# Head gates by one broadcast load, a planner that keeps TensorE's tilings apart, and copies that free PSUM first on VectorE

## The chip, the cores and the metric

The kernel runs on one core of one Trainium2 chip. The metric is the device time of one execution in microseconds (us), the median over several runs. The engines named below are TensorE (PE: matrix products; its weight loads are shown apart as PEld), VectorE (DVE), ScalarE (ACT), GpSimd (POOL) and SyncE (SP, which only issues DMAs and waits). Each engine executes its own instructions strictly in the order in which the program gives them; engines and DMAs wait for one another by semaphores. SBUF is the on-chip memory with 128 partitions, PSUM the accumulator memory that TensorE writes, in banks of 128 x 512 fp32.

## The reference

Two branches read the same x of shape (1, 2048, 512) and are mixed token by token:

```python
g = sigmoid((x * gate_w).sum(-1, keepdims=True))
out = g * A(x) + (1 - g) * B(x)
# B: a gated feed-forward, F = 1792
B = (relu(x @ W_gate) * (x @ W_up)) @ W_down
# A: 32 heads of 16, the sequence cut into 4 segments of 512
for s in range(4):
    a_dot = softmax(q_s k_s^T / 4 + causal mask) v_s
    a_mem = phi(q_s) M / (phi(q_s) z + 1e-6)      # phi(t) = t + 1 if t > 0 else exp(t)
    o_s   = sigmoid(beta) * a_mem + (1 - sigmoid(beta)) * a_dot
    M, z  = M + phi(k_s)^T v_s, z + sum phi(k_s)
A = concat(o_s) @ wo
```

beta has one value per head. Inputs and output are bf16; sums run in fp32.

## The kernel before, in words

**Layout.** Everything is kept transposed, features on partitions: x of a segment is xT (128 x 4 x 512). Two heads share each block of 32 partitions, even and odd ones (r = 0, 1), so that four blocks of 32 (quadrants, j = 0 to 3) times two heads are the eight heads of a chunk c; four chunks make 32 heads. One unit u is one chunk of one segment; there are 16.

**Work of a segment.** Full-array matmuls of 512 columns (helper `matmuls`, L322, in groups of two) make q, k, v, the two feed-forward products g and u (L618, L625), the down product (L638) with the output projection on top (L644). Per unit, attention makes five *fills* of score groups with TensorE's array split into four row blocks of 32 (`qk`, L473, mode "row"); ScalarE takes the exponential of each fill (L494), GpSimd cuts the causal diagonal (L500), and two value groups follow with the array split into four column blocks (`pv`, L513, mode "col"). VectorE transposes and normalises the value groups (L542 to L553), and from segment 1 on adds what the memory M gives (L569, L527). `memory` (L587) updates M from phi(k), which a DMA transposes (L447).

**What frees PSUM.** Eight banks: four hold the scores (sp), four the rest (wb). A q or k matmul group needs one of the four wb banks until VectorE has copied it to QT or kt (L403, L427), and ScalarE has taken its exponential where the memory needs that (L411, L439). v is copied to Vp by ScalarE or VectorE (L463), by the table VACT over the four token tiles. The product h of the feed-forward is made on VectorE from u in PSUM and ScalarE's relu of g (L623, L629) into one of RH = 16 buffers hT, each of which is free again when the down matmuls have read it (hread).

**What sets the order.** The program adds all this as tasks to a planner (`Plan`), with an engine, an assumed duration, a key (the smaller, the more urgent) and the tasks each depends on. The planner plays the engines forward in assumed time: whenever an engine is free, it starts the ready task with the smallest key that finds its PSUM bank. The order that comes out is the order in which instructions are emitted; nothing is decided on the chip. A change of TensorE's mode (None for the full array, "row", "col") adds SWITCH = 100 ns to the task. RL = 40000 is taken off the key of tasks that free PSUM in the feed-forward and in `normalise`. Loads count as arriving by a fixed clock (`arrival`).

**The start.** The loads are issued ahead of all planned work. SP issues half of x of segment 0, half of wq, wk, then gate and up weights, xT of segment 1 by a transposing DMA (L193), and the rest. ScalarE's stream issues the other halves, wv (L203 to L207), then beta (L210, tile betab) in four loads, one for each quadrant, in pieces of two bf16 values, 4 bytes, and last gate_w (L213, tile gw). TensorE runs ten matmuls on zeros (L679), transposes x of segment 0 (L337), and VectorE and ScalarE copy two chunks each to xT (L342). The head gates (`head_gates`, L268) take exp(-beta) (L274) and make 1/(1+e) and e/(1+e) in gcat, laid out by quadrant, so that row 32j holds the two heads of block j for every chunk.

Of the kernel before, what the change touches and what calls it, by code (L numbers as in the profile page):

```python
# [7 lines left out]
BF16 = mybir.dt.bfloat16  # L8
# [4 lines left out]
P = 128  # L13
# [18 lines left out]
class Task:  # L32

# [15 lines left out]
class Plan:  # L49
# [24 lines left out]
    def run(self):  # L74
# [13 lines left out]
        while left:  # L88
            progressed = True
            while progressed:  # L90
                progressed = False
                for t in sorted((t for t in ready if t.avail <= now), key=lambda t: t.key):
                    if busy.get(t.eng, 0.0) > now:
                        continue
                    if t.need is not None and not t.need.banks:
                        got = self.pick(t.need, now)
                        if got is None:
                            continue
                        t.need.banks = got
                        for b in got:  # L100
                            self.free[b] = None
                    if mode.get(t.eng) != t.mode:
                        mode[t.eng] = t.mode
                        t.dur += SWITCH
                    t.start = now
                    busy[t.eng] = now + t.dur
                    t.done = now + t.dur + t.lat
                    order.append(t)
                    ready.remove(t)
                    left -= 1  # L110
                    for s in t.frees:
# [22 lines left out]
def kernel(  # L134
# [37 lines left out]
    betab = sb([P, NC, 2], BF16, "betab")  # L172
# [34 lines left out]
    got_v = load_cols(nc.scalar, wv_sb, A_wv, 0, D)  # L207
    with nc.allow_non_contiguous_dma(reason="1 KB"):
        for j in range(4):
            nc.scalar.dma_start(  # L210
                out=betab[32 * j:32 * j + 32], in_=A_beta.rearrange("(c j r) -> j c r", j=4, r=2)
                [j:j + 1].to_broadcast([32, NC, 2]))
# [51 lines left out]
    eb = sb([P, NC, 2], F32, "eb")  # L264
# [3 lines left out]
    def head_gates():  # L268
        gb = gcat[:, :, 1, :]
        nc.vector.tensor_scalar(gb, eb[:], 1.0, None, ALU.add)  # L270
        nc.vector.reciprocal(gb, gb)
        nc.vector.tensor_tensor(gcat[:, :, 0, :], eb[:], gb, ALU.mult)
# [122 lines left out]
    def proj_q(seg, c):  # L395
# [7 lines left out]
        prj["q", seg, c] = plan.add("DVE", 690, key, lambda: nc.vector.tensor_copy(  # L403
# [9 lines left out]
        prj["pq", seg, c] = plan.add("DVE", 640, key + 500, lambda: phi(  # L413
            pqT[i][:], QT[i][:], e[0][:]), [b, prj["q", seg, c]], DVL)

    def proj_k(seg, c):
# [8 lines left out]
        def cp():  # L425
            kt.append(rpool.tile([P, L], BF16, name="kt"))
            nc.vector.tensor_copy(kt[0][:], bank(sl))  # L427
        d = plan.add("DVE", 690, key, cp, [a], DVL, frees=[sl])
        prj["k", seg, c] = [
            plan.add("DVE", 345, key, lambda: nc.vector.tensor_scalar(  # L430
                KTe[u % RQ][:], kt[0][:], mcol_e[:, 0:1], None, ALU.mult), [d], DVL),
            plan.add("DVE", 345, key + 1, lambda: nc.vector.tensor_scalar(
# [13 lines left out]
        b = plan.add("DVE", 640, key + 500, ph, [b, d], DVL)  # L446
# [35 lines left out]
    def attention(seg, c):  # L482
# [47 lines left out]
        att["ot", u] = plan.add("DVE", 1000 if seg else 660, key, back, [a] + war + (  # L530
# [4 lines left out]
    def normalise(u, m, key, groups):  # L535
# [10 lines left out]
        def part():  # L546
# [10 lines left out]
            "DVE", 1350 if m else 1180, key, part,  # L557
# [20 lines left out]
    def memory(seg):  # L578
# [29 lines left out]
        att["mbd", seg] = plan.add("DVE", 1400, key, up, [a] + war, DVL, frees=[sl])  # L608

    def ffn_tasks(seg):  # L610
        i = seg % 2
        hs = []
        for fv in range(NF):
# [11 lines left out]
            u = matmuls(key + 1, got_x[seg] + [got_u[piece]], usl, proj_mm(wu_sb, fv, seg))  # L625
            if seg == 0:
# [3 lines left out]
                [r, u] + hread.get(NF * seg + fv - RH, []), DVL, frees=[usl]))  # L630
# [26 lines left out]
    VACT = (1, 0, 1, 0)  # L657
# [56 lines left out]
```

## Time and profile before

| What | Value |
|---|---|
| Runs: median of 3 (lowest to highest) | 291.66 us (291.22 to 291.77) |
| The profiled execution: its own time, its span | 291.2 us, 289.3 us |
| Mean granted TensorE clock of it | 0.988 |
| Busy TensorE / weight loads / VectorE / ScalarE / GpSimd | 271.6 / 114.7 / 205.3 / 196.7 / 87.5 us |
| HBM read, written | 8.13 MB, 2.10 MB |

The profile is of one execution. The span runs from its first instruction to its last; the execution's own time has some 2 us more around it. Matmuls overlap one another, so that a busy TensorE isn't TensorE at its peak; the distance between two starts tells more than the length of one (a matmul of 512 columns is shown with 380 ns, while a long row of them advances by about 216 to 219 ns each). A few per cent of the matmul records are missing, so a group of four can be shown as three. In rows of a timeline or a chain, the first number is the start and the second the length in us; "x8" means eight instructions merged; "[0.34 <- X]" is idle time of that engine just before, with what ended it. ACTq and SPq are the streams of ScalarE and SP where they issue DMAs.

### The profile page before, as it was taken

How to read it: one execution, taken by the hardware profiler on the slowest of the kernel's cores; microseconds unless marked ns; L12 is line 12 of the kernel's file. 1: busy time of each engine (PE TensorE's matmuls, PEld its weight loads, DVE VectorE, ACT ScalarE, POOL GpSimd, SP SyncE). 2: the span in 40 equal slices, each digit the busy share in tenths (PEclk: the TensorE clock that was granted, in tenths of full speed). 3: DMA queues.
4: the chain of work that ended last, by engine and by line, in shares of the span. 5: the costliest groups of instructions: out<-in, count | busy, mean ns of one | idle time of the engine just before them, and what ended most of it. 6: DMA issues, size and time to landing. Idle time of an engine off the chain costs nothing.

```text
span 289.3 us, 5294 instructions
## 1 busy us (share of the span) xinstructions
PE 271.6 (94%) x2085; PEld 114.7 (40%) x2122; DVE 205.3 (71%) x423; ACT 196.7 (68%) x176; POOL 87.5 (30%) x144
## 2 busy tenths in 40 slices
PE   8299999999999999999999999999989999999994
PEld 4034343444333443334434344334433433444441
DVE  3076886888888678976999588967799928563211
ACT  0338978888896669978887679889787767533100
POOL 6002424242424351513342534342334243300000
PEclk9689999999999999999999999999999999999999
DMA  7699921001300100000001100000000000000011
GB/s 236 192 267 347 248 57 36 3 0 22 72 18 21 36 20 18 2 18 2 0 20 36 39 20 2 0 2 0 2 0 0 20 19 20 18 2 0 0 36 37
DMA packets 24920, 13.70 MB, mean 47 GB/s; under 512 B 14400, under 2 KB 24896, under 8 KB 24896
## 3 DMA queue, kind: packets, MB, share of 16 engines
q1 hardware_dynamic: 22720, 12.32, 16.3%
q10 hardware_dynamic: 2176, 1.05, 1.3%
q8 instruction: 16, 0.26, 0.4%
q14 instruction: 8, 0.07, 0.1%
HBM read 8.13 MB, written 2.10 MB: 35 GB/s over the span
## 4 chain that ended last, share of the span: by engine, by line
PE 74%; DVE 12%; ACT 6%; issue 3%; DMA 3%; ACTq 1%; POOL 0%; DVEq 0%
PE wb L322 58%; PE sp L473 7%; PE wb L513 6%; DMA wv_sb<-in_A_wv_dram 3%; ACT E L494 3%; DVE T L542 2%; DVE hT L629 2%; DVE QT L403 1%; DVE kt L427 1%; PE wb L587 1%; ACT e L411 1%; PE wb L569 1%; DVE o L553 1%; ACT e L439 1%; DVE cf L551 1%
## 5 line engine op out<-in xcount | busy, mean ns | idle before, releaser
L494 ACT ACTIVATE E<-sp 128x2048 bf16<-128x2048 f32 x80 | 150.4, 1880 | 34.1 <-PE sp L473 24.9
L500 POOL TENSOR_SCALAR_AFFINE_SELECT E<-E 128x512 bf16<-128x512 bf16 x128 | 82.5, 660 | 161.1 <-ACT E L494 161.1
L322 PE MATMUL wb<-xT,wu_sb 128*128 128x512 bf16 x212 | 57.4, 380 | 1.9 <-DVE T L542 0.6
L322 PE MATMUL wb<-xT,wg_sb 128*128 128x512 bf16 x218 | 58.4, 380 | 0.5 <-issue 0.3
L322 PE MATMUL wb<-wd_sb,hT 128*128 128x512 bf16 x215 | 52.0, 380 | 1.8 <-issue 0.8
L629 DVE TENSOR_TENSOR hT<-wb,rg 128x512 bf16<-128x512 f32 x56 | 38.0, 680 | 19.0 <-PE wb L322 11.8
L542 DVE STREAM_TRANSPOSE T<-wb 128x512 f32<-128x512 f32 x56 | 36.7, 693 | 12.1 <-PE wb L513 11.0
L623 ACT ACTIVATE rg<-wb 128x512 bf16<-128x512 f32 x56 | 33.2, 600 | 17.5 <-PE wb L322 17.1
L322 PEld LDWEIGHTS <-hT 128*128 128x128 bf16 x224 | 20.2, 98 | 27.5 <-issue 6.2
L322 PEld LDWEIGHTS <-wu_sb 128*128 128x128 bf16 x224 | 20.1, 98 | 27.0 <-issue 6.6
L322 PEld LDWEIGHTS <-wg_sb 128*128 128x128 bf16 x224 | 20.1, 98 | 25.3 <-issue 4.6
L652 DVE TENSOR_SCALAR osb<-wb,ngcol 128x512 bf16<-128x512 f32 x16 | 11.8, 739 | 20.9 <-PE wb L322 17.6
L322 PE MATMUL wb<-xT,wq_sb 128*128 128x512 bf16 x59 | 17.7, 410 | 5.8 <-ACT xT L342 5.6
L513 PE MATMUL wb<-E,Vp 128*17 128x256 bf16 (+3 forms) x512 | 20.6, 300 | 0.5 <-DVE Vp L463 0.5
L553 DVE TENSOR_TENSOR o<-T,cf 128x512 bf16<-128x512 f32 x28 | 20.1, 719 | 1.0
L403 DVE CAST QT<-wb 128x512 bf16<-128x512 f32 x16 | 10.9, 684 | 12.1 <-PE wb L322 10.5
L473 PE MATMUL sp<-QT,KTo 32*128 32x512 bf16 (+3 forms) x256 | 17.1, 300 | 0.6
L473 PE MATMUL sp<-QT,KTe 32*128 32x512 bf16 (+3 forms) x256 | 17.3, 302 | 0.3
L322 PE MATMUL wb<-xT,wk_sb 128*128 128x512 bf16 x63 | 17.1, 389 | 0.3 <-issue 0.2
L322 PE MATMUL wb<-wv_sb,xT 128*128 128x512 bf16 x63 | 16.4, 380 | 0.1
L513 PEld LDWEIGHTS <-Vp 128*17 128x17 bf16 x512 | 10.9, 91 | 13.5 <-issue 3.8
L322 PE MATMUL wb<-wo_sb,oT 128*128 128x512 bf16 x61 | 16.0, 380 | 0.2 <-issue 0.2
(69 smaller groups left out, 194.8 us busy)
## 6 DMA issues: line engine op xcount, KB each, us to landing
out_dram<-osb SPq DMA_DIRECT2D x16, 128.0 KB, 1.7
wd_sb<-in_B_W_down_dram SPq DMA_DIRECT2D x2, 896.0 KB, 10.1
wg_sb<-in_B_W_gate_dram SPq DMA_DIRECT2D x2, 512.0 KB, 8.8
wu_sb<-in_B_W_up_dram SPq DMA_DIRECT2D x2, 512.0 KB, 9.1
wg_sb<-in_B_W_gate_dram SPq DMA_DIRECT2D x2, 384.0 KB, 4.7
wu_sb<-in_B_W_up_dram SPq DMA_DIRECT2D x2, 384.0 KB, 5.3
wk_sb<-in_A_wk_dram SPq DMA_DIRECT2D x1, 512.0 KB, 7.3
wv_sb<-in_A_wv_dram ACTq DMA_DIRECT2D x1, 512.0 KB, 8.6
```

What stands on the lines that cost most here:

```text
L322: nc.tensor.matmul(bank(sl), lhsT=lhsT, rhs=rhs, start=(start and q == 0), stop=(stop and q == n - 1))
L403: prj["q", seg, c] = plan.add("DVE", 690, key, lambda: nc.vector.tensor_copy(QT[i][:], bank(sl)), [a], DVL, frees=[sl])
L411: nc.scalar.activation(e[0][:], bank(sl), ACT.Exp)
L473: nc.tensor.matmul(sp[:, j, off:off + n], lhsT=kt[32 * j:32 * j + 32, kb * P:(kb + 1) * P], rhs=QT[i][32 * j:32 * j + 32, kb * P:kb * P + ...
L494: b = plan.add("ACT", 1880, key, lambda Ef=Ef: nc.scalar.activation(Ef[:], sp[:], ACT.Exp, scale=SCALE), [a] + eread.get(n - RE, []), ACL)
L500: nc.gpsimd.affine_select(out=m, in_=m, compare_op=ALU.is_ge, fill=0.0, base=0, pattern=[[0, 4], [1, P]], channel_multiplier=-1)
L513: nc.tensor.matmul(wb[sl.banks[0]][32 * j:32 * j + HW, kb * P:kb * P + w], lhsT=Vp[i][:, kb, 8 * c + 2 * j + r, 0:HW], rhs=E[(5 * u + f) % ...
L542: done.append(plan.add("DVE", 700, key - RL, lambda r=r, sl=sl: nc.vector.transpose(T[m][:, r], bank(sl)), [a, att.get(("part", m, u - 1)) ...
L553: nc.vector.tensor_tensor(dst[0].rearrange("p (q r e) -> p r q e", r=2, e=DH), t[:, :, :, 0:DH], cf[:, :, :, None].to_broadcast([P, 2, 16, ...
L623: nc.scalar.activation(rg[0][:], bank(sl), ACT.Relu)
L629: nc.vector.tensor_tensor(hT[(NF * seg + fv) % RH][:], bank(sl), rg[0][:], ALU.mult)),
L652: nc.vector.tensor_scalar(osb[0][:], bank(sl), ngcol[:, tt:tt + 1], None, ALU.mult)
```

## The change

Five things change together.

1. beta is loaded once, as all 32 values (64 bytes) to every one of the 128 partitions. exp(-beta) is taken over 128 x 32, and four VectorE copies, one for each quadrant of 32 partitions, pick that quadrant's 4 x 2 values into a new tile ebq, from which the gates are made as before.
2. The planner ranks a task that would step TensorE from one split of the array directly to the other behind every other ready task, and counts 226 ns in place of 100 ns for such a step. The emitted instructions themselves are the same.
3. The copies of q and k to QT and kt (L403, L427) get a key smaller by RQK = 40000, like the other tasks that free PSUM.
4. In the plan, the up matmul of a feed-forward piece (L625) depends on the down matmuls that read its hT buffer before, where VectorE's product (L628) had depended on them. On the chip VectorE's product still waits for them.
5. Assumed durations of several VectorE tasks are longer, and VACT is swapped: of the four v copies of a segment the first and third now go to VectorE, the second and fourth to ScalarE.

```diff
@@ Plan.run
-                for t in sorted((t for t in ready if t.avail <= now), key=lambda t: t.key):
+                def rank(t):
+                    turn = t.mode and mode.get(t.eng) and t.mode != mode[t.eng]
+                    return (bool(turn), t.key)
+                for t in sorted((t for t in ready if t.avail <= now), key=rank):
...
                     if mode.get(t.eng) != t.mode:
+                        t.dur += SWITCH + (126 if t.mode and mode.get(t.eng) else 0)
                         mode[t.eng] = t.mode
-                        t.dur += SWITCH
@@ the loads
-    betab = sb([P, NC, 2], BF16, "betab")
+    betab = sb([P, H], BF16, "betab")
...
+    nc.scalar.dma_start(out=betab[:], in_=A_beta.partition_broadcast(P))
     with nc.allow_non_contiguous_dma(reason="1 KB"):
-        for j in range(4):
-            nc.scalar.dma_start(
-                out=betab[32 * j:32 * j + 32], in_=A_beta.rearrange("(c j r) -> j c r", j=4, r=2)
-                [j:j + 1].to_broadcast([32, NC, 2]))
         nc.scalar.dma_start(out=gw[:], in_=gate_w.rearrange("(c p) -> p c", p=P))
@@ head gates
-    eb = sb([P, NC, 2], F32, "eb")
+    eb = sb([P, H], F32, "eb")
+    ebq = sb([P, NC, 2], F32, "ebq")
...
     def head_gates():
         gb = gcat[:, :, 1, :]
-        nc.vector.tensor_scalar(gb, eb[:], 1.0, None, ALU.add)
+        for j in range(4):
+            nc.vector.tensor_copy(ebq[32 * j:32 * j + 32], eb.rearrange(
+                "p (c j r) -> p j c r", j=4, r=2)[32 * j:32 * j + 32, j])
+        nc.vector.tensor_scalar(gb, ebq[:], 1.0, None, ALU.add)
         nc.vector.reciprocal(gb, gb)
-        nc.vector.tensor_tensor(gcat[:, :, 0, :], eb[:], gb, ALU.mult)
+        nc.vector.tensor_tensor(gcat[:, :, 0, :], ebq[:], gb, ALU.mult)
@@ proj_q (copy QT, phi), proj_k (copy kt, masked copies KTe and KTo, phi)
-        prj["q", seg, c] = plan.add("DVE", 690, key, lambda: nc.vector.tensor_copy(
+        prj["q", seg, c] = plan.add("DVE", 690, key - RQK, lambda: nc.vector.tensor_copy(
-        prj["pq", seg, c] = plan.add("DVE", 640, key + 500, lambda: phi(
+        prj["pq", seg, c] = plan.add("DVE", 830, key + 500, lambda: phi(
-        d = plan.add("DVE", 690, key, cp, [a], DVL, frees=[sl])
+        d = plan.add("DVE", 690, key - RQK, cp, [a], DVL, frees=[sl])
-            plan.add("DVE", 345, key, lambda: nc.vector.tensor_scalar(
+            plan.add("DVE", 460, key, lambda: nc.vector.tensor_scalar(
-            plan.add("DVE", 345, key + 1, lambda: nc.vector.tensor_scalar(
+            plan.add("DVE", 460, key + 1, lambda: nc.vector.tensor_scalar(
-        b = plan.add("DVE", 640, key + 500, ph, [b, d], DVL)
+        b = plan.add("DVE", 830, key + 500, ph, [b, d], DVL)
@@ longer durations: att["ot"] 1000/660 -> 1210/710, att["part"] 1350/1180 -> 1560/1300, att["mbd"] 1400 -> 1900
@@ ffn_tasks
-            u = matmuls(key + 1, got_x[seg] + [got_u[piece]], usl, proj_mm(wu_sb, fv, seg))
+            u = matmuls(key + 1, got_x[seg] + [got_u[piece]] + hread.get(NF * seg + fv - RH, []),
+                        usl, proj_mm(wu_sb, fv, seg))
...
-                [r, u] + hread.get(NF * seg + fv - RH, []), DVL, frees=[usl]))
+                [r, u], DVL, frees=[usl]))
...
-    VACT = (1, 0, 1, 0)
+    VACT, RQK = (0, 1, 0, 1), 40000.0
```

More of the change, by code (lines that the diff above doesn't have):

```diff
@@ L529, in attention @@
         war = [ffn.get(("o", seg - 2, q)) for q in range(4)]
-        att["ot", u] = plan.add("DVE", 1000 if seg else 660, key, back, [a] + war + (
+        att["ot", u] = plan.add("DVE", 1210 if seg else 710, key, back, [a] + war + (
             [recalled[u][0]] if seg else []), DVL)
@@ L556, in normalise @@
         att["part", m, u] = a = plan.add(
-            "DVE", 1350 if m else 1180, key, part,
+            "DVE", 1560 if m else 1300, key, part,
             done + [att["gate", u // 4], att.get(("ot", u - 2))], DVL)
@@ L607, in memory @@
         war = [att.get(("recall", 4 * seg - 4 + c)) for c in range(NC)]
-        att["mbd", seg] = plan.add("DVE", 1400, key, up, [a] + war, DVL, frees=[sl])
+        att["mbd", seg] = plan.add("DVE", 1900, key, up, [a] + war, DVL, frees=[sl])
     def ffn_tasks(seg):
```

## The prediction

> **What bounds the kernel now.** I read the waits of TensorE first, then the chain that ended last at both its ends, then the start in the order of issue. This is the view of the waits, TensorE's rows (engine, line, releaser: total us, times, longest).
>
> ```profile
> span 289.3 us, 5294 instructions
> ...
> PE wb L322 <- ACT xT L342: 5.6, 1, 5.6
> PE wb L322 <- issue: 1.9, 12, 0.2
> ...
> PE wb L322 <- ACT e L411: 0.8, 2, 0.6
> PE wb L322 <- DVE T L542: 0.6, 1, 0.6
> PE wb L513 <- DVE Vp L463: 0.5, 1, 0.5
> ```
>
> One wait stands out, a single one of 5.6 us. The rows on real releasers behind it come to 0.8 + 0.6 + 0.5 = 1.9 us. The twelve waits called "issue" are at most 0.2 us each, the length of one full matmul, and I read them as matmuls whose records are missing. So from the start phase on TensorE is full. The stretches (us, TensorE busy, weight loads, VectorE, ScalarE, GpSimd, granted clock, DMA share, GB/s) say the same:
>
> ```profile
> 7.00:12.80 5.80, 0.26 (x2) 0.00 (x0) 0.28 (x1) 1.90 (x3) 0.00 (x0) 0.75 0.65 196
> 12.80:17.20 4.40, 4.38 (x12) 1.66 (x12) 1.38 (x2) 0.45 (x1) 0.00 (x0) 0.55 0.95 286
> 17.50:285.40 267.90, 260.91 (x2046) 109.92 (x2081) 200.30 (x405) 194.39 (x173) 82.46 (x128) 1.00 0.14 35
> ```
>
> From 17.5 to 285.4 TensorE is the bound (260.9 of 267.9 us, all at full clock); VectorE (200.3) and ScalarE (194.4) have room. Ahead of it lie 5.8 us in which TensorE stands, and 4.4 us in which it runs with a clock of 0.55. Because TensorE executes one fixed order, whatever starts that dense part earlier moves the end by as much, unless an input is then late.
>
> Who holds the start? The chain, in order of time (start, length, what):
>
> ```profile
> 1.86 8.59 DMA wv_sb<-in_A_wv_dram
> 10.46 0.39 ACTq L213
> 10.89 1.28 ACT L342
> 12.18 0.59 ACT xT L342
> 12.82 4.47 PE wb L322 x11
> ...
> 273.53 10.74 PE wb L322 x49
> ```
>
> ScalarE's stream cannot issue the load of gw (L213) until wv has landed at 1.86 + 8.59 = 10.45. Behind that issue stand the table load (1.28 us) and ScalarE's two copies of transposed x, and the second q matmul waits for the first copy. The last row gives the pitch of a full matmul, 10.74 / 49 = 0.219 us.
>
> Why does gw wait for wv? From the timeline and the table of DMA issues (there the last number is us to landing):
>
> ```profile
> 0.80 0.48 ACTq L201 DMA_DIRECT2D E<-in_A_x_dram  x1
> 1.30 0.52 ACTq L201 DMA_DIRECT2D wq_sb<-in_A_wq_dram  x1
> 1.82 0.46 SPq L184 DMA_DIRECT2D wk_sb<-in_A_wk_dram  x1
> 2.38 0.55 ACTq L210 DMA_DIRECT2D betab<-in_A_beta_dram  x1
> 4.47 0.32 ACTq L210 DMA_DIRECT2D betab<-in_A_beta_dram  x1
> 5.97 0.32 ACTq L210 DMA_DIRECT2D betab<-in_A_beta_dram  x1
> 11.69 7.00 SPq L193 DMA_TRANSPOSE xT<-in_A_x_dram  x1
> ...
> wk_sb<-in_A_wk_dram SPq DMA_DIRECT2D x1, 512.0 KB, 7.3
> E<-in_A_x_dram ACTq DMA_DIRECT2D x1, 256.0 KB, 3.7
> wq_sb<-in_A_wq_dram ACTq DMA_DIRECT2D x1, 256.0 KB, 4.6
> xT<-in_A_x_dram SPq DMA_TRANSPOSE x3, 9.1
> gw<-in_gate_w_dram ACTq DMA_DIRECT2D x1, 1.0 KB, 7.5
> ```
>
> Eight loads of both queues go out by 2.4 us without a wait. After that each issue falls on the landing of an earlier one, in turn: betab's second piece at 4.47 on x (0.80 + 3.7 = 4.5), its fourth at 5.97 on wq (1.30 + 4.6 = 5.9), gw on wv. So there are eight places, taken in turn, and three extra betab loads push gw back to the place of wv.
>
> **The change part by part.** *One betab load in place of four.* gw moves from behind the fourth betab load to behind the only one. It is then the ninth or tenth issue of both queues and waits for a half of x: about 4.5 us (bounds: 4.5, and 10.46 if it still gets wv's place). Then 0.39 + 1.28 lead to 6.2. Here are TensorE's rows of the start that are needed from now on:
>
> ```profile
> 6.88 0.38 PE L322 MATMUL wb<-xT,wq_sb 128*128 128x512 bf16 x1
> 17.54 2.17 PE L322 MATMUL wb<-wv_sb,xT 128*128 128x512 bf16 x8
> 22.56 0.55 PE L355 MATMUL wb<-gw,xT 128*128 128x1 bf16 x16
> 25.99 1.04 PE L322 MATMUL wb<-xT,wq_sb 128*128 128x512 bf16 x3
> ```
>
> The transposes end near 6.9, so ScalarE's copies now end at about 7.2 and 7.8 (0.59 each), and the second half of the eight q matmuls is free. The fourth q matmul runs at 7.8, the eighth ends at 7.8 + 5 x 0.219 = 8.9. The k weights land at 1.82 + 7.3 = 9.12. Six k matmuls come ahead of v now: 9.12 + 6 x 0.219 = 10.43. wv lands at 10.45. So v starts at about 10.47 in place of 17.54: **-7.07 us**. That is more than the wait of 5.6, because the matmul at 6.88 still took 0.38 us, a warm one, while those after the wait ran at a clock of 0.55; without the long wait the array need not cool. Lower bound of the gain: 5.6 (the wait alone), or nothing where gw keeps its place.
>
> By the Trainium skill (TensorE: Matmul & The Clock Gate, Part 1) the clock is set by windows of about 3.4 us that run freely, and an idle window cools it. The trace agrees, with 5.6 us idle and then 0.55. By that rule the short waits that I expect (0.2 to 0.4 us) leave the array warm, and the sum stays as it is.
>
> What is late next? Two loads. gw is read at 22.56, after the shift at 15.5. Its 7.5 us from issue to landing now begin behind wv and one betab load; the worst is 10.45 + 7.5 = 18.0, a wait of 2.5 us, the best none. I take 0, because three quarters of betab's pieces no longer stand ahead of it. The next segment's xT, loaded at 11.69, landed near 11.69 + 9.1 = 20.8 and is read first by the q matmuls at 25.99 (the row after q, k, v of segment 0), after the shift at 18.9. If it did not move, TensorE would wait 1.9 us. The stretches say that it moves:
>
> ```profile
> 2.00:9.00 7.00, 5.26 (x26) 2.70 (x25) 1.96 (x7) 0.00 (x0) 3.78 (x9) 1.00 1.03 333
> 9.00:15.00 6.00, 2.18 (x6) 0.81 (x6) 0.69 (x1) 2.36 (x3) 0.00 (x0) 0.58 0.54 159
> ```
>
> While betab's four-byte pieces land, the loads fall from 333 to 159 GB/s: 6 x 174 = 1.0 MB not moved, 3.1 us at the full rate. One load with 64 bytes a partition has a quarter of the pieces. SP also issues its loads earlier, since three places come free. Bounds for xT's landing: 17.7 (all 3.1 us back) and 20.8; I take 19.3, a wait of **+0.4 us** (0 to 1.9).
>
> *Four copies on VectorE and an exponential over 32 columns.* No such copy stands in the trace; the nearest rows are these:
>
> ```profile
> L244 DVE MEMSET mcol_e<- 16x1 f32 x4 | 0.2, 59 | 0.2
> ...
> L272 DVE TENSOR_TENSOR gcat<-eb,gcat 128x8 f32<-128x8 f32 x1 | 0.2, 168 | 0.0
> ```
>
> Four copies cost 4 x 59 to 4 x 168 ns, 0.24 to 0.67 us, and I take 0.5: they are nearest to the second row. Queued behind them on VectorE are copies of k and v; they lie once, at the start, beside the k, v and gate matmuls. Priced at **0**; without that cover 0.5.
>
> *No step from one tiling to another.* In the order before, a score group (row tiling, L473) follows a value group (column tiling, L513) directly eight times, first at 96.98 and last at 237.68. Compare the price of a step:
>
> ```profile
> 96.98 0.40 PE L473 MATMUL sp<-QT,KTo 32*128 32x512 bf16 x4
> ...
> 237.03 0.72 PE L513 MATMUL wb<-E,Vp 128*17 128x512 bf16 x16
> 237.68 0.40 PE L473 MATMUL sp<-QT,KTo 32*128 32x512 bf16 x4
> ...
> 36.28 0.72 PE L513 MATMUL wb<-E,Vp 128*17 128x512 bf16 x16
> 36.93 0.39 PE L322 MATMUL wb<-xT,wg_sb 128*128 128x512 bf16 x1
> ```
>
> Both value groups stream 512 + 384 + 256 + 128 = 1280 columns, 2.5 full matmuls, 0.55 us. The direct step takes 0.65 - 0.55 = 0.10 us, the step back to the full array the same 0.65 - 0.55 = 0.10. So a direct step is not dearer, and full matmuls put between make two steps of one: 8 x 0.10 = **+0.8 us** (0 where none was ready to go between, 1.6 if score groups split up further). The plan's new 126 ns penalty is not in this trace.
>
> The Trainium skill (TensorEngine Tiling (Array Packing), Key Properties) says that changing the tiling mode drains TensorE. By it, too, the detour pays twice where the direct step pays once; it gives no size, and the sum stays.
>
> *Copies of q and k first on VectorE, longer durations in the plan, up matmuls planned behind the reads of hT, v copies swapped between ScalarE and VectorE.* These only change orders. What they can win is the waits of TensorE on the other engines, 1.9 us in all by the first view, and by the same size they can lose: a copy that now goes first makes a transpose or a product on VectorE 0.7 us later. VectorE has 200 of 268 us, so I take **-0.3** (-1.9 to +1.9).
>
> Sum: -7.07 + 0.4 + 0.8 - 0.3 = -6.2. The profiled execution took 291.2 us (span 289.3), which gives 285.0; the runs' median of 291.66 lies 0.46 above that execution, so I forecast 285.2 for a median.
>
> **The rivals.** *Inputs bind after the earlier start.* gw or xT lands as late as the bounds allow and TensorE waits 1.9 to 2.5 us in place of 0.4: about 287. For it: xT is needed within half a microsecond of the landing that I took. Against it: less small traffic ahead of it. *The array is cold all the same.* If the short waits cool it, the start pays 4.4 x 0.45 = 2.0 us again: 287.2. Against it speaks the warm matmul at 6.88. *The new order also clears most of TensorE's later waits,* -1.9 in place of -0.3, and half the detours prove unneeded: 285.2 - 1.6 - 0.4 = 283.2. Against it: the waits are single ones at scattered places. *The start does not move, and the change is slower.* If gw still takes the place of wv, ScalarE's copies stay at 12.2, nothing is won, and the detours remain: 291.2 + 0.8 = 292.0. This decides from where gw is issued later than about 9.7, since every microsecond ahead of 10.46 is worth one. For it: the places are given out in an order that the trace shows only once. Against it: three issues fewer move gw up by four places in that count.
>
> **How the numbers follow.** Likeliest 285.2, chance 0.62, own range 283.6 to 286.5. Late inputs 0.16, cold array 0.05, better order 0.11, start unmoved 0.06. The range from 282.8 to 288.0 takes in all but the last, and some of the ends of the others. A measurement here tells 0.2% (0.6 us) from no change. Slower 0.05 comes from the unmoved start, same 0.03 from that case and from a pile of lost orders, faster 0.92 from all the rest.
>
> **What would show it.** The steps are right if the wait of TensorE on ScalarE's xT copy shrinks from 5.6 us to under 0.6, if gw is issued near 4.5, if the first v matmul starts at 10.3 to 11.0 at a clock of 1.00, and if the dense part is about as long as before, 268 us plus 0.5. A wait of TensorE at the next segment's first q matmul or at the gate matmuls shows the late inputs. The tiling step is right if no score group follows a value group directly and the steps number eight more, at 0.10 us each. The forecast is wrong if gw is issued after 6 us, or if the dense part grows or shrinks by more than 2 us.

## The result: 282.17 us, and the profile after

The changed kernel took 282.17 us (median of four runs, 282.02 to 282.55), the kernel before on the same chip 291.44 us (290.62 to 291.77): a ratio of 0.9688, with a 95% interval of 0.9665 to 0.9711. The forecast was 285.2, its range 282.8 to 288.0. The sign and the main cause were right, and the gain was larger than the range allowed. The profiled execution took 282.55 us against 291.2 before, 8.65 less.

First the page of the kernel after (span; busy us, share and instructions by engine; granted clock by slices of the span):

```profile
span 280.8 us, 5327 instructions
...
PE 272.8 (97%) x2122; PEld 113.4 (40%) x2122; DVE 205.7 (73%) x427; ACT 196.6 (70%) x176; POOL 87.6 (31%) x144
...
PEclk9999999999999999999999999999999999999999
```

The span is 8.5 us shorter and TensorE's clock is full in every slice. Now the timeline of the kernel after, TensorE's rows of the start with three rows of ScalarE and two of VectorE (start, length, what):

```profile
4.47 0.38 ACTq L214 DMA_DIRECT2D gw<-in_gate_w_dram  x1
4.88 1.28 ACT L347 ACT_TABLE_LOAD   x1 [4.88 <-DMA E<-in_A_x_dram]
6.17 1.07 ACT L347 COPY xT<-wb 128x512 bf16<-128x512 bf16 x2
6.35 2.19 PE L327 MATMUL wb<-xT,wq_sb 128*128 128x512 bf16 x8
9.55 1.47 PE L327 MATMUL wb<-xT,wk_sb 128*128 128x512 bf16 x6 [1.01 <-DMA wk_sb<-in_A_wk_dram]
10.96 2.06 PE L327 MATMUL wb<-wv_sb,xT 128*128 128x512 bf16 x8
15.44 0.54 PE L360 MATMUL wb<-gw,xT 128*128 128x1 bf16 x16
17.03 0.68 DVE L273 COPY ebq<-eb 32x8 f32<-32x8 f32 x4
19.27 1.04 PE L327 MATMUL wb<-xT,wq_sb 128*128 128x512 bf16 x4
276.90 0.75 DVE L658 TENSOR_SCALAR osb<-wb,ngcol 128x512 bf16<-128x512 f32 x1 [3.13 <-PE wb L327]
```

The load of gw goes out at 4.47 in place of 10.46, on the landing of a half of x. ScalarE's copies follow at 6.17, the eight q matmuls run warm from 6.35, and TensorE stands only 1.01 us for wk. The first v matmul starts at 10.96; before it was 17.54. The last line is the output's last step on VectorE. In the kernel before, that line was

```profile
285.39 0.75 DVE L652 TENSOR_SCALAR osb<-wb,ngcol 128x512 bf16<-128x512 f32 x1 [3.13 <-PE wb L322]
```

These two points, the first v matmul and the last osb, cut the time in two, and everything below uses them. Up to the first v matmul lies the *start*: 17.54 before, 10.96 after, **-6.58**. From there to the last osb lies the *dense part*: 285.39 - 17.54 = 267.85 before, 276.90 - 10.96 = 265.94 after, **-1.91**. Together -8.49, the shift of the span. So three quarters of the gain came from the start, as forecast, and a quarter from the dense part, which the forecast had 0.9 us longer.

TensorE's waits of the kernel after (line and tile, releaser: us in total, times, longest; its L327, L478, L518 and L547 are L322, L473, L513 and L542 of before):

```profile
PE wb L685 <- DVE mcol_e L243: 1.3, 1, 1.3
PE sp L478 <- ACT E L499: 1.1, 2, 0.8
PE wb L327 <- DMA wk_sb<-in_A_wk_dram: 1.0, 1, 1.0
PE wb L327 <- ACT rg L628: 0.4, 1, 0.4
PE wb L327 <- DVE T L547: 0.2, 1, 0.2
```

The first and third belong to the start; 1.1 + 0.4 + 0.2 = 1.7 us lie in the dense part. For the dense part before, the prediction had summed three rows to 1.9 us. The view has three more there:

```profile
PE wb L322 <- ACT e L439: 0.3, 1, 0.3
PE wb L569 <- DVE QT L403: 0.3, 1, 0.3
PE wb L322 <- DVE kt L427: 0.2, 1, 0.2
```

With them it is 1.9 + 0.8 = 2.7 us, in seven waits, and most are longer than shown. Two of them in the timeline of before:

```profile
43.85 1.04 PE L322 MATMUL wb<-xT,wg_sb 128*128 128x512 bf16 x4
45.23 1.02 PE L322 MATMUL wb<-xT,wu_sb 128*128 128x512 bf16 x4 [0.34 <-ACT e L439]
...
213.73 0.60 PE L569 MATMUL wb<-pqT,mbd 128*128 128x512 bf16 x2
214.91 0.59 PE L322 MATMUL wb<-xT,wu_sb 128*128 128x512 bf16 x2 [0.59 <-DVE T L542]
```

Four matmuls from 43.85 on, at 0.216 us each, leave room for the next at 44.71; it started at 45.23, 0.51 us late, where the row shows 0.34. At 213.73 two leave room at 214.16; the next started 0.75 late, shown as 0.59. The reason is the shown length of a full matmul, 0.38 us, which is 0.16 more than the pitch: idle time is counted from the shown end. So a wait between two full matmuls is shown about 0.16 short, and one under 0.16 not at all; behind a step to another tiling the loss is smaller. Worked out from the starts, with the gaps of one matmul's length taken as missing records, TensorE's waits in the dense part come to about 4.7 to 5.1 us before and 2.5 after.

The other views: the stretches (us, TensorE busy, weight loads, VectorE, ScalarE, GpSimd, granted clock, DMA share, GB/s) of before, then of after.

```profile
9.00:14.00 5.00, 1.18 (x3) 0.41 (x3) 0.00 (x0) 2.36 (x3) 0.00 (x0) 0.59 0.44 118
```

```profile
9.00:14.00 5.00, 4.45 (x22) 1.67 (x23) 2.95 (x8) 1.66 (x4) 0.00 (x0) 1.00 1.00 305
10.96:276.70 265.74, 264.04 (x2083) 109.83 (x2082) 200.50 (x408) 194.21 (x173) 82.55 (x128) 1.00 0.16 41
```

With one beta load the loads move 305 GB/s where they moved 118.

### The profile page after: what moved, and what is told of

Same layout as the page of the kernel before. It is cut to its first block, busy times and chain, and to the rows that moved or that the text cites. A ratio compares the mean times of both kernels' runs of the same rounds, so it can differ in the third digit from the quotient of the medians.

```text
span 280.8 us, 5327 instructions
## 1 busy us (share of the span) xinstructions
PE 272.8 (97%) x2122; PEld 113.4 (40%) x2122; DVE 205.7 (73%) x427; ACT 196.6 (70%) x176; POOL 87.6 (31%) x144
## 3 DMA queue, kind: packets, MB, share of 16 engines
q10 hardware_dynamic: 1744, 1.06, 1.3%
## 4 chain that ended last, share of the span: by engine, by line
PE 92%; ACT 3%; DMA 3%; DVE 1%; issue 0%; SPq 0%; ACTq 0%
PE wb L327 73%; PE sp L478 9%; PE wb L518 7%; DMA wk_sb<-in_A_wk_dram 3%; ACT E L499 2%; PE wb L574 2%; PE wb L592 1%; ACT rg L628 1%; PE wb L360 1%; SPq L204 0%; DVE osb L658 0%; DVE T L547 0%; PE wb L380 0%; ACT e L416 0%; ACTq L628 0%
## 5 line engine op out<-in xcount | busy, mean ns | idle before, releaser
L327 PE MATMUL wb<-xT,wg_sb 128*128 128x512 bf16 x224 | 59.7, 380 | 0.0
L327 PE MATMUL wb<-xT,wu_sb 128*128 128x512 bf16 x224 | 59.3, 380 | 0.4 <-ACT rg L628 0.4
L327 PE MATMUL wb<-wd_sb,hT 128*128 128x512 bf16 x224 | 54.1, 380 | 0.0
L547 DVE STREAM_TRANSPOSE T<-wb 128x512 f32<-128x512 f32 x56 | 36.7, 693 | 14.9 <-PE wb L518 9.0
L628 ACT ACTIVATE rg<-wb 128x512 bf16<-128x512 f32 x56 | 33.0, 602 | 13.8 <-PE wb L327 13.8
L327 PEld LDWEIGHTS <-hT 128*128 128x128 bf16 x224 | 20.4, 98 | 26.1 <-issue 4.2
L327 PEld LDWEIGHTS <-wu_sb 128*128 128x128 bf16 x224 | 20.3, 98 | 26.2 <-issue 5.0
L327 PEld LDWEIGHTS <-wg_sb 128*128 128x128 bf16 x224 | 19.8, 98 | 25.3 <-issue 5.5
L518 PE MATMUL wb<-E,Vp 128*17 128x256 bf16 (+3 forms) x512 | 20.4, 300 | 0.0
L478 PE MATMUL sp<-QT,KTo 32*128 32x512 bf16 (+3 forms) x256 | 17.1, 299 | 0.8 <-ACT E L499 0.8
L478 PE MATMUL sp<-QT,KTe 32*128 32x512 bf16 (+3 forms) x256 | 17.3, 302 | 0.3 <-ACT E L499 0.3
L327 PE MATMUL wb<-xT,wk_sb 128*128 128x512 bf16 x64 | 16.5, 380 | 1.0 <-DMA wk_sb<-in_A_wk_dram 1.0
L327 PE MATMUL wb<-wo_sb,oT 128*128 128x512 bf16 x64 | 17.1, 380 | 0.0
L327 PE MATMUL wb<-wv_sb,xT 128*128 128x512 bf16 x64 | 16.8, 380 | 0.2 <-DVE T L547 0.2
L327 PE MATMUL wb<-xT,wq_sb 128*128 128x512 bf16 x64 | 16.7, 380 | 0.1
L518 PEld LDWEIGHTS <-Vp 128*17 128x17 bf16 x512 | 10.7, 91 | 13.0 <-issue 4.2
```

The source lines that it names most:

```text
L327: nc.tensor.matmul(bank(sl), lhsT=lhsT, rhs=rhs, start=(start and q == 0), stop=(stop and q == n - 1))
L478: nc.tensor.matmul(sp[:, j, off:off + n], lhsT=kt[32 * j:32 * j + 32, kb * P:(kb + 1) * P], rhs=QT[i][32 * j:32 * j + 32, kb * P:kb * P + ...
L518: nc.tensor.matmul(wb[sl.banks[0]][32 * j:32 * j + HW, kb * P:kb * P + w], lhsT=Vp[i][:, kb, 8 * c + 2 * j + r, 0:HW], rhs=E[(5 * u + f) % ...
L547: done.append(plan.add("DVE", 700, key - RL, lambda r=r, sl=sl: nc.vector.transpose(T[m][:, r], bank(sl)), [a, att.get(("part", m, u - 1)) ...
L628: nc.scalar.activation(rg[0][:], bank(sl), ACT.Relu)
```

## The experiments

In the tables, "start" is where the first v matmul begins, "dense" the time from there to the last osb, both of the profiled execution, "xT" what TensorE is shown to wait for the next segment's xT in it, and "net" dense less that wait. Ratios are to the kernel before, run on the same chip.

### Loads alone, orders alone, and the place of gw

The first kernel is the kernel before with the one beta load and its four copies, and the old order:

```diff
-    betab = sb([P, NC, 2], BF16, "betab")
+    betab = sb([P, H], BF16, "betab")
+    nc.scalar.dma_start(out=betab[:], in_=A_beta.partition_broadcast(P))
-        for j in range(4):
-            nc.scalar.dma_start(
-                out=betab[32 * j:32 * j + 32], in_=A_beta.rearrange("(c j r) -> j c r", j=4, r=2)
-                [j:j + 1].to_broadcast([32, NC, 2]))
...
+        for j in range(4):
+            nc.vector.tensor_copy(ebq[32 * j:32 * j + 32], eb.rearrange(
+                "p (c j r) -> p j c r", j=4, r=2)[32 * j:32 * j + 32, j])
```

> The kernel before with the one betab load and the four small copies alone; TensorE's order stays as before. Theory A (the start and the order are two separate gains): TensorE's first v matmul moves from 17.54 to about 10.96 as in the changed kernel, 6.6 us, and the dense part from there to the last output projection stays at about 266.8 us: 284.9 us in all. Rival B (the order is worth nothing, and TensorE's waits were a consequence of the late start): the dense part shrinks by itself to about 265 and the time comes near 282.5. Rival C (the earlier start is paid back later, since loads are now late in the old order): 286.5 or more.

The second is the kernel after with the four old loads back in place of these lines, and so the new order alone.

> The changed kernel with the four old betab loads: only the orders differ from the kernel before. Theory A: the start stays as before (first v matmul near 17.5), the dense part is as short as in the changed kernel, 264.9 in place of 266.8 us: 289.5 us. Rival B (the order is worth nothing): 291.4, or 292.1 with the seven more tiling steps.

The third is the kernel after with three useless broadcast loads of beta ahead of gw, which push it back by three places and leave everything else alone:

```diff
+    more = sb([P, 3, H], BF16, "more")
+    for j in range(3):
+        nc.scalar.dma_start(out=more[:, j, :], in_=A_beta.partition_broadcast(P))
     with nc.allow_non_contiguous_dma(reason="1 KB"):
         nc.scalar.dma_start(out=gw[:], in_=gate_w.rearrange("(c p) -> p c", p=P))
```

> The changed kernel with three more broadcast loads of beta (64 bytes a partition, to a tile that nobody reads) between betab's and gate_w's, so that gate_w's load is again the eighth of ScalarE's stream. Theory P (gate_w's issue takes the place of an earlier load and waits for its landing): gw is issued near 10.5 again, the second q matmul waits as before, the clock falls, the first v matmul starts near 17.5, the time is 288.7 us. Rival Q (the four-byte pieces made the start slow): the issue of gw and the start stay as in the changed kernel, 282.2 to 283.

| Kernel | median us | ratio (95%) | start | dense | xT | net |
|---|---|---|---|---|---|---|
| before | 291.44 | 1 | 17.54 | 267.84 | | 267.84 |
| loads alone | 285.6 | 0.9804 (0.9782 to 0.9826) | 10.48 | 268.75 | 0.92 | 267.83 |
| orders alone | 289.57 | 0.9941 (0.9918 to 0.9964) | 18.42 | 265.90 | | 265.90 |
| after | 282.17 | 0.9688 (0.9665 to 0.9711) | 10.96 | 265.94 | | 265.94 |
| after, three more loads | 289.05 | 0.9926 (0.9905 to 0.9947) | 16.62 | 266.04 | | 266.04 |

The loads alone came 0.7 us above theory A's 284.9 (B had 282.5): the profiled execution, at 285.01, holds the late xT below and a start at 10.48, and of the three slower ones there is no trace. The orders alone came at A's 289.5, and the three more loads 0.35 above the 288.7 of the theory of gw's place. By the parts the two halves add up: the loads move the start and leave the dense part as it was (267.83 net against 267.84), and the orders take 1.9 us off the dense part and don't help the start. By the medians they fall short, 2.0% and 0.6% against 3.1%, which is some 1.7 us. Two differences of about that size together can be seen: the 0.92 of xT, and a start that came 0.88 us later with the orders alone, where TensorE's clock returned later (its mean from 16 to 18 us is 0.50 there and 0.81 before).

And it is gw's place that makes the start late. Slower loads are no rival, because wv lands at 10.45 before and near 10.9 after (9.1 us from its issue at 1.86): a gw in wv's place would go out that late in either. The timeline of the kernel with three more loads:

```profile
4.42 1.79 ACTq L215 DMA_DIRECT2D more<-in_A_beta_dram  x3
9.94 0.39 ACTq L217 DMA_DIRECT2D gw<-in_gate_w_dram  x1
10.35 1.28 ACT L350 ACT_TABLE_LOAD   x1 [10.35 <-DMA more<-in_A_beta_dram]
12.28 3.15 PE L330 MATMUL wb<-xT,wq_sb 128*128 128x512 bf16 x7 [5.66 <-ACT xT L350]
16.62 2.17 PE L330 MATMUL wb<-wv_sb,xT 128*128 128x512 bf16 x8
```

gw is issued at 9.94, the wait of 5.6 us is back as 5.66, and with it all of the late start.

With the loads alone, a wait that the kernel before did not have shows up. Its timeline:

```profile
19.90 1.04 PE L323 MATMUL wb<-xT,wq_sb 128*128 128x512 bf16 x3 [0.92 <-DMA xT<-in_A_x_dram]
```

This is the late xT of the rival "inputs bind". It lies in the kernel after as well, only not in every execution: in the one profiled first the same matmuls start at 19.27 without a wait.

### One part of the order undone at a time

Each of these is the kernel after less one part. No ranking of tiling steps, and the plain 100 ns:

```diff
-                for t in sorted((t for t in ready if t.avail <= now), key=rank):
+                for t in sorted((t for t in ready if t.avail <= now), key=lambda t: t.key):
-                        t.dur += SWITCH + (126 if t.mode and mode.get(t.eng) else 0)
+                        t.dur += SWITCH
```

> The changed kernel without the planner's rank and without the 126 ns penalty: its emitted order has 188 changes of tiling in place of 193, 8 of them direct from one split to the other (1 in the changed kernel). Theory A (every step costs 0.10 us, a direct one too): 0.5 us less of steps, so 281.7 if the waits stay as they are. Rival D (a direct step costs 0.226 us, as the plan has it): 7 x 0.126 = 0.9 more for the direct steps, less 0.5: 282.6 us.

Copies of q and k with their old keys (RQK = 0.0); the old assumed durations of VectorE's tasks; the wait for the hT buffer back on VectorE's product in the plan; and VACT = (1, 0, 1, 0); in this order:

> The changed kernel with RQK = 0: copies of q and k have their old keys; 195 tiling steps. Theory R (copies that free PSUM first are what removed TensorE's waits): the 2.6 us of waits that left the dense part come back, 284.8 us, with waits on VectorE's copies of q or k in TensorE's rows. Rival S (the waits depend on how the whole order falls, and no part owns them): within 1 us of 282.2 either way, plus 0.2 for two more steps.

> The changed kernel with the old, shorter assumed durations of VectorE's tasks; 194 tiling steps. Theory T (the plan came closer to the chip, so fewer instructions stand ahead of work that isn't ready): 2 us or more of waits come back, 284.2 or more, as waits of TensorE on VectorE. Rival S: within 1 us of 282.2.

> The changed kernel with the reads of hT planned ahead of VectorE's product again, not of the up matmul; 193 tiling steps. On the chip the product waits for them in both. I expect little, within 0.5 us of 282.2; a rival has the up matmuls now hold a PSUM bank while the product waits: 283.5 or more.

> The changed kernel with the old table of which engine copies v; 196 tiling steps, 0.3 us more. Theory R and T: 282.2 to 282.8, since neither says anything of it. Rival S (any change of the order moves the waits): off by more than 1 us, with waits in places that have nothing to do with v.

And the kernel after once more, unchanged, on another chip:

> The changed kernel once more, beside the three that follow. The last profiles show that the next segment's xT lands near 18.4 us in the changed kernel, and near 19.9 in five others with an equally early start, where TensorE waits 0.9 to 1.2 us for it. If that differs from execution to execution, some executions here take 283.5 us and others 282.2. If it belongs to the changed kernel's order, all take 282.2.

| Kernel | median us | ratio (95%) | start | dense | xT | net |
|---|---|---|---|---|---|---|
| after, again | 283.08 | 0.9709 (0.9683 to 0.9736) | 10.39 | 267.19 | 1.07 | 266.12 |
| no ranking | 284.15 | 0.9757 (0.9739 to 0.9774) | 10.27 | 268.19 | 1.17 | 267.02 |
| old keys of copies | 284.24 | 0.9768 (0.9750 to 0.9786) | 10.27 | 267.73 | 1.10 | 266.63 |
| old durations | 283.47 | 0.9731 (0.9704 to 0.9757) | 10.41 | 265.84 | | 265.84 |
| old place of hT's wait | 283.77 | 0.9754 (0.9737 to 0.9771) | 10.43 | 267.41 | 1.03 | 266.38 |
| old VACT | 283.57 | 0.9737 (0.9716 to 0.9758) | 10.27 | 268.03 | 1.32 | 266.71 |

No forecast for these kernels could be right to half a microsecond: five of the six profiled executions of this table had the late xT, the unchanged kernel's too (in the view of its waits):

```profile
PE wb L327 <- DMA xT<-in_A_x_dram: 1.1, 1, 1.1
```

The kernel with the old durations shows both faces. Its profiled execution had no such wait and took 282.04 us; its three others, of which there is no trace, took 283.44 to 283.59. So without the ranking neither 281.7 nor 282.6 came out but 284.15, and 284.24 without the keys lies between the 284.8 and 282.2 of the two theories without deciding for either: an unchanged kernel stands at 283.08. Nor is 283.77 with the old place of hT's wait a sign for its rival of 283.5 or more, since 1.03 of it is xT. Net of xT the order of after repeats within 0.2 us (265.90 to 266.12 in the executions so far), and against it the ranking is worth about 1.0, VACT 0.7, the keys 0.6, hT's place 0.4 and the durations nothing. These do not add: they come to 2.7 us, where the whole order is worth 1.9, so some parts clear the same waits. All of it had to be seen again without the late xT.

### xT out of the way, by another order of loads

wk and wv are loaded in halves from both queues, betab and gw go to SP's queue, and xT of segment 1 is issued ahead of the second half of the gate and up weights:

```diff
-    got_k = [load_cols(nc.sync, wk_sb, A_wk, 0, D)] * 2
-    got_v = load_cols(nc.scalar, wv_sb, A_wv, 0, D)
-    nc.scalar.dma_start(out=betab[:], in_=A_beta.partition_broadcast(P))
-    with nc.allow_non_contiguous_dma(reason="1 KB"):
-        nc.scalar.dma_start(out=gw[:], in_=gate_w.rearrange("(c p) -> p c", p=P))
+    got_k = [load_halves(wk_sb, A_wk, NC, D * D * 2)] * 2
+    got_v = load_halves(wv_sb, A_wv, NC, D * D * 2)
...
+    nc.sync.dma_start(out=betab[:], in_=A_beta.partition_broadcast(P))
+    with nc.allow_non_contiguous_dma(reason="1 KB"):
+        nc.sync.dma_start(out=gw[:], in_=gate_w.rearrange("(c p) -> p c", p=P))
+    nc.sync.dma_start_transpose(out=xT[1][:], in_=x[L:2 * L, :])
```

> The changed kernel's order of work on every engine, with the loads issued in another order: wk and wv in halves from both queues, beta and gate_w from SP behind the first gate and up weights, and the next segment's xT ahead of the second ones. Then ScalarE's stream issues only four loads and waits for none. If the start is bound by the landing of wk (9.5) and wv (10.9), as the changed kernel's profile says, the k weights land near 7.5, the v weights near 9, the first v matmul starts near 9.5 in place of 10.96, xT is never late, and the time is 280.7 us. If TensorE's own work or gw is the bound from there on, 282.

The same without the ranking, and the same with the whole order of before:

> As the one before, but with the planner's old rank and its old price for a step between tilings; xT is out of the way here. If the rank's worth is real apart from xT: the run without the rank had 2.24 us more in its dense part than the changed kernel, 1.2 of them the wait for xT, so 281.7 us here. If steps alone counted, 280.2.

> The same loads with the order of the kernel before on every engine (beta's one load and the four copies kept). The run with the beta load alone had a dense part of 268.3 us, 0.9 of them the wait for xT, against 265.5 in the changed kernel; so 1.9 us above the first of these three, 282.6. If the order's gain came from xT and the start, 280.7.

| Kernel | median us | ratio (95%) | start | dense |
|---|---|---|---|---|
| these loads, order of after | 282.31 | 0.9687 (0.9660 to 0.9714) | 9.68 | 266.88 |
| no ranking | 283.22 | 0.9714 (0.9690 to 0.9737) | 9.40 | 267.96 |
| order of before | 284.88 | 0.9774 (0.9751 to 0.9797) | 10.11 | 269.32 |

xT is no longer waited for, and the first starts 0.7 to 1.3 us earlier than the kernel after did in its three profiles (10.39 to 10.96), but it came at 282.31, not at the 280.7 expected: betab now lands late, and the exponential of beta holds up ScalarE, whose v copies stand behind it. ScalarE's row in the timeline of the first:

```profile
13.04 0.23 ACT L280 ACTIVATE eb<-betab 128x32 f32<-128x32 bf16 x1 [2.27 <-DMA betab<-in_A_beta_dram]
```

A small load that nobody on the path needs blocked an engine that the path does need. That costs the dense part 0.9 us (266.88 against 266.0), and 1.5 us with the order of before (269.32 against the 267.83 of the loads alone); so that kernel stands 2.6 us above the first, where 1.9 was expected. The ranking's worth is the same as above: 267.96 - 266.88 = 1.1 in the dense part, 0.9 in the medians.

So betab went back to ScalarE's queue, behind its halves of the weights:

```diff
+    nc.scalar.dma_start(out=betab[:], in_=A_beta.partition_broadcast(P))
-    nc.sync.dma_start(out=betab[:], in_=A_beta.partition_broadcast(P))
```

> The changed kernel's order of work; wk and wv in halves from both queues, beta's load last on ScalarE's queue, gate_w on SP behind the first gate and up weights, the next segment's xT ahead of the second ones. The run before it had beta's load on SP, where it landed at 13.0 us and ScalarE waited 2.3 us for it; here it lands near 10. So the waits of TensorE behind that (0.2 and 0.4 us) go, the first v matmul starts near 9.7, and the dense part is 265.6: 281.5 us, faster than the changed kernel's 282.2 to 283.1.

On these loads, again one part less each: the keys of the copies, VACT, the ranking, and then the whole order of before.

> As i4_beta_act with RQK = 0. On the changed kernel the dense part without the wait for xT grew from 265.5 to 266.1. So 0.6 us above i4_beta_act if that part owns it; 2 or more if the copies' priority is the main cause.

> As i4_beta_act with the old table for the v copies. On the changed kernel the dense part without the wait for xT grew by 0.8 us, so 0.8 us above i4_beta_act; near 0 if the table has no worth of its own.

> As i4_beta_act without the rank and the 126 ns. With beta's load on SP the same change cost 0.9 us, with 5 steps less. So 0.9 us above i4_beta_act if the rank has this worth in any company; 0.5 below it if steps alone counted.

> The loads of i4_beta_act with the order of the kernel before on every engine (the rank, the priorities, the durations, the place of the up matmuls and the table of the v copies all undone). If the whole order is worth what the dense parts say (267.4 without xT against 265.6), 1.8 us above i4_beta_act: 283.9 us, with TensorE's rows showing again the waits on the exponentials, the transposes and the v copies. If the parts simply add (0.0 + 0.3 + 0.3), 282.7.

Beside the last one, on its chip, ran the kernel after for a third time:

> The changed kernel a third time: executions with a late xT near 283.4 us, the others near 282.2, so a median between these, and on average no faster than the 282.05 of i4_beta_act.

| Kernel | median us | ratio (95%) | start | dense | xT |
|---|---|---|---|---|---|
| new loads, order of after | 282.05 | 0.9683 (0.9661 to 0.9704) | 10.45 | 266.06 | |
| old keys of copies | 282.08 | 0.9690 (0.9665 to 0.9715) | 9.58 | 266.57 | |
| old VACT | 282.34 | 0.9697 (0.9673 to 0.9720) | 10.43 | 266.65 | |
| no ranking | 282.35 | 0.9696 (0.9675 to 0.9717) | 9.97 | 266.95 | |
| order of before | 283.53 | 0.9735 (0.9719 to 0.9751) | 10.12 | 267.74 | |
| kernel after, third time | 283.52 | 0.9735 (0.9720 to 0.9749) | 10.62 | 266.93 | 0.95 |

The first came at 282.05, half a microsecond above the 281.5 expected, and the order of before at 283.53 (283.9 expected). With xT out of the way that order is 267.74 - 266.06 = 1.7 us longer in the dense part and 1.5 us in the ratios (0.0052 of 291.3; two chips). Its waits are those of the kernel before. TensorE's waits with the new loads and the old order, and then with the order of after:

```profile
PE wb L324 <- ACT e L413: 0.8, 2, 0.6
PE wb L324 <- DVE T L544: 0.6, 1, 0.6
PE wb L515 <- DVE Vp L465: 0.5, 1, 0.5
...
PE wb L324 <- ACT e L441: 0.3, 1, 0.3
PE wb L571 <- DVE QT L405: 0.3, 1, 0.3
PE wb L324 <- DVE kt L429: 0.2, 1, 0.2
```

```profile
PE sp L479 <- ACT E L500: 1.1, 2, 0.8
PE wb L328 <- ACT rg L629: 0.4, 1, 0.4
PE wb L328 <- DVE T L548: 0.2, 1, 0.2
```

Without the ranking alone:

```profile
PE sp L476 <- ACT E L497: 1.3, 2, 0.8
...
PE wb L325 <- DVE T L545: 0.6, 1, 0.6
PE wb L325 <- DVE hT L633: 0.4, 1, 0.4
PE wb L325 <- ACT rg L626: 0.4, 1, 0.4
```

The single parts show 0.5, 0.6 and 0.9 us in the dense part, close to the 0.6, 0.7 and 1.0 of the other loads, while the medians show 0.0, 0.3 and 0.3, with intervals of 0.6 to 0.7 us to either side. Part of the difference is the start, which moved between executions by more than these effects with the same code ahead of it (below). I take the dense parts for the better measure, since two arrangements of loads agree on them. How much each part is worth stays open between the two sets of numbers; the worth of the whole does not.

As a kernel, the new loads at 282.05 us are no slower than the kernel after in any pairing and faster than it was the third time (0.9704, the upper end, against 0.9720, the lower end); from its first time (0.9688) it can't be told apart. They were not run on the same chip.

## Why the prediction was right or wrong

**The start: right, -6.58 for -7.07.** gw was issued at 4.47 (4.5 forecast), v began at 10.96 inside the band of 10.3 to 11.0 at a clock of 1.00, and the wait on ScalarE's xT copy is gone from the waits. The half microsecond is two loads, wk and wv. By the chain of the kernel after, and its row among the DMA issues for wv (the last number is us to landing),

```profile
1.82 7.68 DMA wk_sb<-in_A_wk_dram
9.55 3.47 PE wb L327 x14
...
wv_sb<-in_A_wv_dram ACTq DMA_DIRECT2D x1, 512.0 KB, 9.1
```

wk landed at 9.50, not 9.12, so that six k matmuls at 0.216 from 9.55 end at 10.85, and wv landed near 10.9, not 10.45. That one beta load in place of four does it was shown by the loads alone, and that gw's place is the reason by the three more loads. The rival of an unmoved start (292.0) fell, and so did the cold array: the wait of 1.01 us for wk left the clock at 1.00.

**gw and the copies: right.** gw is read at 15.44 without a wait. The four copies took 0.68 us, at the upper bound of 0.67, and nothing waited for them.

**xT: right in size, wrong in kind.** I took one wait of 0.4 us. In fact there are two cases: none, as in the first profile and in that of the old durations, or 0.92 to 1.32 us, as in seven others. Both lie within the bounds of 0 and 1.9. It is about as much as the 0.9 and 1.35 us by which the kernel after stood higher the second and third time. What decides between the cases was not found: the load was issued at 10.93 in the first profile, without the wait, and at 10.21 in one with it, so a late issue is not it. The loads' rate did come back as I took it (305 GB/s for 118), though the four-byte size of beta's pieces, to which I had put the fall, is not the reason (below).

**The steps of tiling: right as a price.** Seven more steps in place of eight (193 against 186, counted in the emitted order; one step from columns straight to rows is left where there were eight), and a direct step shows the same 98 to 99 ns as one back to the full array, in the kernel without the ranking too. That is +0.7 for +0.8. The plan's extra 126 ns has no counterpart in any trace here. Yet the ranking pays: the full matmuls that it sets between a value group and a score group cover waits that come back without it (hT 0.4, T 0.6 for 0.2, the exponential 1.3 for 1.1), and its sum is -0.9, not +0.8. I had priced what the ranking adds and not what it moves.

**The orders: the step that failed.** "What they can win is the waits of TensorE on the other engines, 1.9 us in all by the first view [...] so I take -0.3 (-1.9 to +1.9)." The waits shrank by about 2.6 us: the dense part is 1.9 shorter although it has 0.7 us more of tiling steps. That -2.6, ranking included, stands where the sum had -0.3, and it is beyond the bound. The bound was wrong for two reasons that the profile of before held ready: I summed three rows of the waits and left out three small ones (0.8 us), and the view shows a wait between full matmuls 0.16 us short and the shortest not at all. By starts the pool was 4.7 to 5.1 us. And the value was wrong because I drew it between gain and loss without a reason for either.

With what was measured, the sum is -6.58 + 0 + 0.7 - 2.6 = -8.5, and the last osb moved by -8.49. That it closes proves nothing, since the -2.6 is what the dense part leaves over; the waits counted by starts give 2.2 to 2.6 by themselves. The rival "better order" had the mechanism, at 283.2: its -1.9 carried the same short bound.

**The last half microsecond: chance.** The sum gave 285.0 for the profiled execution, which took 282.55. For the median I went up by 0.2 (the 0.46 that I had named would have made 285.5, and I gave no reason for taking less), and the median came 0.38 below that execution instead. On two other chips the same kernel took 283.08 and 283.52, inside the range. The number would have looked right there, with the orders mis-sized all the same: net of xT the dense parts are 266.12 and 265.98.

## What to carry to other kernels

Split a change by a point in the trace that every version has (here the first v matmul) and compare the parts, net of a wait that comes and goes; the totals mix effects that have nothing to do with each other. Where an engine is pipelined, work out its waits from starts and pitch, and sum all the rows before calling the sum a bound. Ahead of a load that an engine's own stream issues, count the loads that are still under way: a small one more can hold up the engine's next computation by microseconds.

## What the runs showed of the hardware that I had not expected

**Loads of beta slow the loads beside them, in pieces of 4 bytes and of 64.** The kernel before loads beta in four loads of 32 x 4 = 128 pieces of 4 bytes; the kernel with three more loads has four of 128 pieces of 64 bytes. Its stretch, and then one of the kernel after:

```profile
9.00:14.00 5.00, 1.72 (x5) 0.62 (x5) 0.24 (x1) 2.36 (x3) 0.00 (x0) 0.50 0.48 129
```

```profile
10.00:13.00 3.00, 3.00 (x17) 1.03 (x15) 2.24 (x6) 0.71 (x2) 0.00 (x0) 1.00 1.06 324
```

129 GB/s against 118 before and 305 after: with pieces of 64 bytes the loads are as slow as with those of 4. I had put the fall down to four-byte pieces. In five microseconds that is (305 - 129) x 5 = 0.9 MB less. The number of small pieces alone is not the reason either: gate_w comes in 512 pieces of 2 bytes, as many as the four loads of beta have, and most of them move between 10 and 13 us in the kernel after, at 324 GB/s. In beta's loads many partitions read the same few bytes; whether that is it was not tried. In both slow stretches the DMA engines are shown busy for less than half of the time (0.44 and 0.48), and what held them stays open.

**The warm-up moves from run to run.** The 16 transposes ahead of q, in the kernel after, in the one with the new loads, and in the same without the keys, whose code is the same up to there as the second's:

```profile
5.45 1.06 PE L342 MATMUL wb<-ident,E 128*128 128x128 bf16 x16
```

```profile
5.49 1.91 PE L343 MATMUL wb<-ident,E 128*128 128x128 bf16 x16
```

```profile
5.06 1.06 PE L343 MATMUL wb<-ident,E 128*128 128x128 bf16 x16
```

1.06 or 1.91 us, and a start at 9.58 or 10.45, for the same instructions: in the second the transposes follow one another every 0.107 us, in the others every 0.055. The traces' record of the granted clock shows the step to full speed at 5.39, 7.28 and 4.60 us in these three, and between 4.09 and 7.23 in the others. This is why an arrangement of loads that allows 9.6 doesn't give it every time. The Trainium skill (TensorE: Matmul & The Clock Gate, Part 1) says that the clock is set by windows of about 3.4 us that run freely and do not start anew with the kernel. The traces agree: in the kernel before the clock steps at 6.51, 9.92 and 16.75 us, 3.41 and 2 x 3.41 apart.
